# Retention and two feed-forward layers on one core: the double-bank PSUM tiles get a pool of their own, and four single-bank tiles follow them

## The chip, the cores and the metric

The kernel runs on one core of a Trainium2 chip. The metric is the time of one execution on the device in microseconds (us). Several runs are given by their median, and the profile is of one execution.

## What is computed

The reference, cut to what matters:

```python
def _attn_ref(q, k, v):                       # 4 x 8 x 576 x 64, fp32
    scores = (1.0 / np.sqrt(D_)) * np.matmul(q, k.transpose(0, 1, 3, 2))
    gamma = 1.0 - 2.0 ** (-5.0 - np.arange(H, dtype=np.float32))
    Dmat = np.where(rel >= 0, gamma[:, None, None] ** rel[None, :, :], 0.0)
    return np.matmul(scores * Dmat[None, :, :, :], v)
...
x = attn_out.transpose(0, 2, 1, 3).reshape(B * S, H * D)      # 2304 x 512
h = x @ w_in;  x = (h * (1.0 / (1.0 + np.exp(-h)))) @ w_out   # layer 1, 512 -> 2048 -> 512
h = x @ w_in2; g = np.maximum(h, 0.0) + alpha * np.minimum(h, 0.0)
out = g @ w_out2                                              # layer 2
```

## The kernel before

Retention (an attention with a fixed decay in place of a softmax) is worked out in 18 blocks of 128 rows, with a state that is carried from block to block. The two layers then take the 2304 rows as three pieces of 768, each in two halves of 384 columns. fp32 values are split into a high and a low part (`split`), and each product is three matmuls of parts.

The layers run in 24 steps: 8 groups of hidden features (`GROUPS`, four for each layer) times the three pieces. The first two steps are interleaved with the last blocks of retention; `close_att` closes retention's pools after them, and the 22 steps after it are the layers alone. A step has two calls of `unit`, each of which forms two blocks of 128 hidden features for both halves by a scheme of Strassen's kind with seven products instead of eight. A product is 6 matmuls of 384 columns. In the order of the code they are A11 (into a tile a), S1 (into d), A12 (a), S2 (b), S4 (d), S3 (b) and A22 (b). Between them the kernel reads partial sums out: ScalarE (ACT) copies a into b after A11, d into s5 after S1, b into s2 after S2; VectorE (DVE) adds s2 to d after S4, and reads b after S3; `activate` reads a, d, s5 and b. Between the products of `unit` the calls `fill(...)` put pieces of the second matmul (`y_pieces` in layer 1, `out_pieces` in layer 2), which accumulate into a tile o and are added to `ybuf` by DVE or copied there by ACT.

PSUM has eight banks of 2 KiB for each partition. Four of them are tiles of one bank (`banks`). The other four are two tiles of two banks each, `xo` and `sd` (`two`), which retention uses whole. `homes` says which places a, b, d and o rotate through; `close_att` appends the halves of `sd` to b and d and the halves of `xo` to o:

```python
    homes = {"a": banks[0:1], "b": banks[1:2], "d": banks[2:3], "o": banks[3:4]}
    ...
        homes["b"].append(two["sd"][:, 0])
        homes["d"].append(two["sd"][:, 1])
        homes["o"] += [two["xo"][:, i] for i in range(2)]
```

So from `close_att` on, every second unit has b and d in the two halves of `sd`, and o goes round banks[3] and the halves of `xo`.

The order of the instructions on each engine is set by the class `Program`: all calls are recorded first, and `order` lists them by estimated start times. PE's order stays as it is written. Dependences are kept by PSUM bank there (`grains`). The semaphores that hold the engines to the data's order are put in by the framework afterwards, from the tiles that each instruction reads and writes. All operations are issued by one helper line, L222, so rows of the profile are told apart by their tiles.

Of the kernel before, what the change touches and what calls it, by code (L numbers as in the profile page):

```python
# [9 lines left out]
F32 = mybir.dt.float32  # L10
# [8 lines left out]
P = 128  # L19
# [206 lines left out]
def retention_ffn_kernel(ctx: ExitStack, tc: tile.TileContext, qkv, w1, w2, alpha, small, out):  # L226
# [4 lines left out]
    ps = ctx.enter_context(tc.tile_pool(name="ps", bufs=1, space=bass.MemoryType.PSUM))  # L231
# [43 lines left out]
    rings["act"].grow(big, "act", HALF, 7)  # L275
    xops = [big.tile([P, 4 * HALF], F32R, name=f"xop{i}") for i in range(7)]
    banks = [ps.tile([P, 512], F32, name=f"bank{i}") for i in range(4)]
    two = {k: ps.tile([P, 2 * 512], F32, name=k).rearrange("p (b t) -> p b t", b=2) for k in ("xo", "sd")}
    homes = {"a": banks[0:1], "b": banks[1:2], "d": banks[2:3], "o": banks[3:4]}

    att_pool = ctx.enter_context(ExitStack())
    att = att_pool.enter_context(tc.tile_pool(name="att", bufs=1))
    packs = [att.tile([P, 4 * DM], F32, name=f"pack{i}") for i in range(PACKS)]
    late_x = ybuf[:, (NPR - 1) * NC * 2 * HALF:]
    packs.append(late_x[:, 0:4 * DM])
# [14 lines left out]
    def close_att():  # L300
        nc.issue()
        att_pool.close()
        pool = ctx.enter_context(tc.tile_pool(name="layers", bufs=1))
        rings["w0"].grow(pool, "w0b_", 14 * 2 * P, 1, F32R)
        rings["w1"].grow(pool, "w1b_", 512, 6, F32R)
        stock.free += [pool.tile([P, HALF], F32R, name=f"gb{i}") for i in range(6)]
        rings["act"].grow(pool, "actb", HALF, 3)
        rings["raw"].grow(pool, "rawb", 512, 1, I64)
        homes["b"].append(two["sd"][:, 0])
        homes["d"].append(two["sd"][:, 1])  # L310
        homes["o"] += [two["xo"][:, i] for i in range(2)]

    def pack(n):
        at = n % (PACKS + 1) if n < EARLY else (n - EARLY) % PACKS
# [376 lines left out]
    for n, (gi, layer, qs, p) in enumerate(steps):  # L691
# [14 lines left out]
        if with_blocks:  # L706
            weights(0, 0)
            if n == 0:
                begin_banks()
            old, queue[:] = queue[:], more_blocks(BPP // 2)  # L710
            for i, e in enumerate(old):
                queue.insert(2 * i, e)
            unit(layer, qs[0], (gi, p), fill, (1, 1, 1, 1, 1, len(queue)))
            queue += more_blocks(BPP // 2)
            unit(layer, qs[1], (gi, p), fill, (0, 1, 0, 1, 0, 1))
            if n == NPR - 2:
                close_att()
                begin_banks()
                nc.sync.dma_start(out=alpha_sb, in_=alpha)
                nc.vector.tensor_scalar(out=nalpha_sb, in0=alpha_sb, scalar1=-1.0, scalar2=1.0, op0=ALU.mult,  # L720
                                        op1=ALU.add)
            else:
                homes["o"].append(banks[0])
            queue += now
            fill(len(queue))
            queue += then
            if n < NPR - 2:
                del homes["o"][1:]
            continue
# [68 lines left out]
```

## Time and profile before

| | |
|---|---|
| median of 3 runs | 929.79 us (929.47 to 930.74) |
| the profiled execution | 929.9 us, of which the span of its instructions is 928.0 us |
| PE busy | 836.5 us (90%) |
| DVE busy | 566.1 us (61%) |
| ACT busy | 487.6 us (53%) |
| DMA queue of the program | 45.7% of 16 engines' time |

PE is TensorE's matmul stream and PEld its weight loads, which run beside it. Matmuls are pipelined, so the rows of two neighbours overlap. Where a row has a time in brackets with an arrow, the engine sat idle that long before it, and the arrow names the engine and tile whose work ended the wait.

### The profile page before, as it was taken

What the parts mean: (1) busy time and instruction counts of PE and PEld (TensorE: products, weight loads), DVE (VectorE), ACT (ScalarE), POOL (GpSimd) and SP (SyncE); (2) the same over time, 40 slices, a digit from 0 to 9 for tenths busy, and PEclk for the clock granted to TensorE, in tenths of its full rate; (3) what the DMA queues carried; (4) which work ended last, traced back from release to release, by engine and by line L of the source; (5) the groups of instructions that cost most, each with busy time, mean ns of one, the idle gap of its engine ahead of it and who ended that gap; (6) DMA issues with size and microseconds to landing.
All of it is one profiled execution on the core that took longest, in us unless ns stands there. A gap on an engine that the chain in (4) does not pass through costs nothing.

```text
span 928.0 us, 15112 instructions
## 1 busy us (share of the span) xinstructions
PE 836.5 (90%) x6222; PEld 755.9 (81%) x6222; DVE 566.1 (61%) x985; ACT 487.6 (53%) x910; POOL 0.2 (0%) x4
## 2 busy tenths in 40 slices
PE   4778999898998999999998998998998998998998
PEld 3667989898998998988997887887886887887886
DVE  5799768767266533763266887685466843643533
ACT  2657468887456633574364677785245632432331
POOL 0000000000000000000000000000000000000000
PEclk9689999999999999999999999999999999999999
DMA  8786738265603851163632645254601733024711
GB/s 328 274 331 212 287 134 304 91 221 213 269 1 98 321 183 56 46 242 142 227 146 94 262 148 203 69 218 179 238 1 45 283 111 128 1 100 183 283 46 69
DMA packets 35637, 157.49 MB, mean 170 GB/s; under 512 B 4080, under 2 KB 4336, under 8 KB 35568
## 3 DMA queue, kind: packets, MB, share of 16 engines
q1 hardware_dynamic: 35568, 156.52, 45.7%
q8 instruction: 49, 0.80, 0.3%
q14 instruction: 20, 0.16, 0.1%
HBM read 118.76 MB, written 37.75 MB: 169 GB/s over the span
## 4 chain that ended last, share of the span: by engine, by line
PE 85%; DVE 5%; ACT 5%; DMA 3%; issue 2%; SPq 0%; DVEq 0%; ACTq 0%
PE bank L222 39%; PE xo L222 29%; PE sd L222 16%; DMA rawb<-in_w 2%; DVE ybuf L222 2%; ACT act L222 1%; ACT sd L222 1%; DMA pack<-in_qkv 1%; ACT ybuf L222 1%; ACT actb L222 1%; DVE act L222 0%; DVE actb L222 0%; ACT top L222 0%; DVE sd L222 0%; ACT low L222 0%
## 5 line engine op out<-in xcount | busy, mean ns | idle before, releaser
L222 PE MATMUL bank<-xop,w 128*128 128x384 f32 x997 | 197.5, 338 | 4.6 <-DVE act L222 3.4
L222 PEld LDWEIGHTS bank<-xop,w 128*128 128x128 f32 x997 | 175.6, 189 | 10.9 <-DVE act L222 2.3
L222 PE MATMUL sd<-xop,w 128*128 128x384 f32 x391 | 87.2, 348 | 21.9 <-ACT act L222 7.8
L222 DVE TENSOR_TENSOR ybuf<-xo,ybuf 128x384 f32<-128x384 f32 (+2 forms) x85 | 52.0, 612 | 83.0 <-PE xo L222 83.0
L222 PEld LDWEIGHTS sd<-xop,w 128*128 128x128 f32 x391 | 67.0, 188 | 36.8 <-ACT act L222 13.8
L222 PE MATMUL xo<-w,g 128*128 128x512 f32 (+1 forms) x273 | 71.8, 392 | 4.7 <-DVE ybuf L222 4.7
L222 PE MATMUL sd<-xop,w0b 128*128 128x384 f32 x270 | 60.8, 349 | 15.9 <-ACT sd L222 5.0
L222 PE MATMUL xo<-g,w 128*128 128x384 f32 x315 | 66.7, 338 | 5.7 <-DVE ybuf L222 3.9
L222 PE MATMUL bank<-xop,w0b 128*128 128x384 f32 x360 | 70.9, 335 | 0.0
L222 DVE TENSOR_TENSOR g<-act,g 128x384 fp32r<-128x384 f32 x103 | 56.6, 553 | 22.9 <-ACT g L222 22.4
L222 PEld LDWEIGHTS sd<-xop,w0b 128*128 128x128 f32 x270 | 46.3, 188 | 27.0 <-ACT act L222 8.0
L222 PEld LDWEIGHTS bank<-xop,w0b 128*128 128x128 f32 x360 | 63.6, 188 | 1.9
L222 ACT CAST g<-act 128x384 fp32r<-128x384 f32 x103 | 52.7, 513 | 20.8 <-DVE act L222 19.2
L222 PEld LDWEIGHTS xo<-g,w 128*128 128x128 f32 x315 | 55.2, 188 | 8.9 <-DVE ybuf L222 5.8
L222 PEld LDWEIGHTS xo<-w,g 128*128 128x128 f32 x273 | 49.8, 188 | 15.1 <-DVE ybuf L222 7.3
L222 ACT ACTIVATE act<-bank 128x384 f32<-128x384 f32 x66 | 32.4, 491 | 53.5 <-PE bank L222 42.1
L222 PE MATMUL bank<-g,w 128*128 128x384 f32 x273 | 56.3, 344 | 1.6 <-DVE g L222 1.5
L222 PEld LDWEIGHTS bank<-g,w 128*128 128x128 f32 x273 | 49.1, 193 | 2.9 <-DVE g L222 2.3
L222 PE MATMUL xo<-w1b,g 128*128 128x512 f32 x168 | 45.3, 397 | 4.4 <-DVE ybuf L222 2.4
L222 ACT COPY ybuf<-xo 128x256 f32<-128x256 f32 (+2 forms) x58 | 25.2, 434 | 39.8 <-PE xo L222 38.3
L222 PE MATMUL xo<-g,w1b 128*128 128x384 f32 x204 | 44.1, 336 | 2.0 <-DVE ybuf L222 2.0
L222 ACT ACTIVATE low<-low,seven 128x512 int32<-128x512 f32 x64 | 44.7, 720 | 0.3
(109 smaller groups left out, 1383.1 us busy)
## 6 DMA issues: line engine op xcount, KB each, us to landing
xop<-od SPq DMA_DIRECT2D x84, 768.0 KB, 6.5
od<-xop SPq DMA_DIRECT2D x42, 768.0 KB, 4.3
pack<-in_qkv SPq DMA_DIRECT2D x32, 512.0 KB, 6.2
raw<-in_w SPq DMA_DIRECT2D x32, 512.0 KB, 4.4
rawb<-in_w SPq DMA_DIRECT2D x28, 512.0 KB, 4.1
out<-ybuf SPq DMA_DIRECT2D x17, 256.0 KB, 2.0
ybuf<-in_qkv SPq DMA_DIRECT2D x4, 512.0 KB, 8.7
ybuf<-in_w SPq DMA_DIRECT2D x4, 512.0 KB, 8.8
```

Source lines behind the costliest of these rows:

```text
L222: getattr(getattr(self.nc, name), method)(*args, **kwargs)
```

## The change

`xo` and `sd` come from a new PSUM pool, which is opened and closed together with retention's buffers. When it has been closed, `close_att` opens another pool with four tiles of one bank each, `late0` to `late3`, and appends those to b, d, o and o.

```diff
     banks = [ps.tile([P, 512], F32, name=f"bank{i}") for i in range(4)]
-    two = {k: ps.tile([P, 2 * 512], F32, name=k).rearrange("p (b t) -> p b t", b=2) for k in ("xo", "sd")}
     homes = {"a": banks[0:1], "b": banks[1:2], "d": banks[2:3], "o": banks[3:4]}
...
     att = att_pool.enter_context(tc.tile_pool(name="att", bufs=1))
+    att_ps = att_pool.enter_context(tc.tile_pool(name="att_ps", bufs=1, space=bass.MemoryType.PSUM))
+    two = {k: att_ps.tile([P, 2 * 512], F32, name=k).rearrange("p (b t) -> p b t", b=2) for k in ("xo", "sd")}
...
-        homes["b"].append(two["sd"][:, 0])
-        homes["d"].append(two["sd"][:, 1])
-        homes["o"] += [two["xo"][:, i] for i in range(2)]
+        late_ps = ctx.enter_context(tc.tile_pool(name="late_ps", bufs=1, space=bass.MemoryType.PSUM))
+        for i, k in enumerate("bdoo"):
+            homes[k].append(late_ps.tile([P, 512], F32, name=f"late{i}"))
```

The order of the instructions stays as it was on every engine; what differs are the semaphores that they wait for. The pieces below are rows of PE, with the waits named, from the step that the profile of before shows from 811 us on: w0b holds the weights, xop_154 is the operand of S1, xop_155 of A12, xop_156 of S2, xop_157 of S4 and xop_158 of S3; the numbers behind a name only tell buffers apart. In the changed program late_1927 is b, late_1928 is d, late_1929 and late_1930 are o. A wait names the engine, not the instruction, and one that an engine has already waited out isn't named again.

PE at A11 (bank_160), S1 and the piece after it, before:

```order
L222 MATMUL bank_160<-xop_153,w0b_1903 128x384 x6
L222 MATMUL sd<-xop_154,w0b_1903 128x384 x2
L222 MATMUL sd<-xop_154,w0b_1903 128x384 [waits Activation_49]
L222 MATMUL sd<-xop_154,w0b_1903 128x384 x3
L222 MATMUL xo<-w_6_128,gb_1910 128x512 [waits DVE_49]
L222 MATMUL xo<-w_7_129,gb_1910 128x512
```

and in the changed program, up to A12:

```order
L222 MATMUL bank_160<-xop_153,w0b_1907 128x384 x6
L222 MATMUL late_1928<-xop_154,w0b_1907 128x384 x6
L222 MATMUL late_1929<-w_6_128,gb_1914 128x512 [waits DVE_49]
L222 MATMUL late_1929<-w_7_129,gb_1914 128x512
L222 MATMUL late_1929<-w_6_128,gb_1915 128x512
L222 MATMUL late_1929<-w1b_1908,g_134 128x512
L222 MATMUL late_1929<-w1b_1909,g_134 128x512
L222 MATMUL late_1929<-w1b_1908,g_135 128x512
L222 MATMUL bank_160<-xop_155,w0b_1907 128x384 [waits Activation_49]
```

S1's third matmul waited for ACT; now S1 is one row, and the wait for ACT's copy out of bank_160 stands where A12 writes that bank again.

PE at S2 and S4, before, and in the changed program:

```order
L222 MATMUL sd<-xop_156,w0b_1903 128x384 [waits Activation_49]
L222 MATMUL sd<-xop_156,w0b_1903 128x384 x5
L222 MATMUL sd<-xop_157,w0b_1903 128x384 x2
L222 MATMUL sd<-xop_157,w0b_1903 128x384 [waits Activation_49]
L222 MATMUL sd<-xop_157,w0b_1903 128x384 x3
```

```order
L222 MATMUL late_1927<-xop_156,w0b_1907 128x384 x6
L222 MATMUL late_1928<-xop_157,w0b_1907 128x384 [waits Activation_49]
L222 MATMUL late_1928<-xop_157,w0b_1907 128x384 x5
L222 MATMUL late_1930<-w_6_128,gb_1914 128x512 [waits DVE_49]
L222 MATMUL late_1930<-w_7_129,gb_1914 128x512
```

S4's third matmul waited for ACT's copy out of b; now only its first one waits, for ACT's earlier copy out of d.

PE at S3 and up to A22 (xop_159), before, and in the changed program:

```order
L222 MATMUL sd<-xop_158,w0b_1903 128x384 [waits Activation_49]
L222 MATMUL sd<-xop_158,w0b_1903 128x384 [waits DVE_49]
L222 MATMUL sd<-xop_158,w0b_1903 128x384 x4
L222 MATMUL xo<-w1b_1906,g_140 128x512
L222 MATMUL xo<-w1b_1907,g_140 128x512
L222 MATMUL xo<-w1b_1906,g_141 128x512
L222 MATMUL xo<-w1b_1908,g_132 128x512
L222 MATMUL xo<-w1b_1909,g_132 128x512
L222 MATMUL xo<-w1b_1908,g_133 128x512
L222 MATMUL sd<-xop_159,w0b_1903 128x384 [waits DVE_49]
```

```order
L222 MATMUL late_1927<-xop_158,w0b_1907 128x384 [waits Activation_49]
L222 MATMUL late_1927<-xop_158,w0b_1907 128x384 x5
L222 MATMUL late_1930<-w1b_1910,g_140 128x512
L222 MATMUL late_1930<-w1b_1911,g_140 128x512
L222 MATMUL late_1930<-w1b_1910,g_141 128x512
L222 MATMUL late_1930<-w1b_1912,g_132 128x512
L222 MATMUL late_1930<-w1b_1913,g_132 128x512
L222 MATMUL late_1930<-w1b_1912,g_133 128x512
L222 MATMUL late_1927<-xop_159,w0b_1907 128x384 [waits DVE_49]
```

S3's second matmul waited for DVE's activation, which reads d; now its first one waits for ACT's copy out of b alone. The wait for DVE ahead of A22 is there in both: DVE reads b after S3.

## Rows read from the trace of the kernel before

**Rows 1.** The page: span, and the granted clock in 40 slices.

```profile
span 928.0 us, 15112 instructions
...
PEclk9689999999999999999999999999999999999999
```

**Rows 2.** Stretches: length, PE, PEld, DVE, ACT, POOL busy (instructions), clock, DMA share, GB/s.

```profile
133.00:220.00 87.00, 80.34 (x445) 76.22 (x444) 62.53 (x107) 70.44 (x127) 0.00 (x0) 1.00 0.60 218
155.00:175.00 20.00, 18.78 (x106) 17.85 (x105) 17.41 (x32) 18.31 (x35) 0.00 (x0) 1.00 0.32 106
470.00:570.00 100.00, 92.42 (x475) 83.12 (x474) 79.01 (x127) 64.16 (x114) 0.00 (x0) 1.00 0.49 187
540.00:560.00 20.00, 19.22 (x96) 17.02 (x95) 18.54 (x30) 15.96 (x29) 0.00 (x0) 1.00 0.57 198
812.00:847.00 35.00, 32.53 (x156) 27.94 (x156) 15.86 (x27) 11.15 (x24) 0.00 (x0) 1.00 0.48 175
133.00:928.00 795.00, 733.43 (x3784) 662.69 (x3782) 466.07 (x813) 417.91 (x772) 0.00 (x0) 1.00 0.42 154
```

**Rows 3.** PE's waits, 133 to 928 us: total us, times, longest.

```profile
PE xo L222 <- DVE ybuf L222: 15.6, 22, 0.8
PE sd L222 <- ACT act L222: 12.6, 24, 0.6
PE sd L222 <- ACT sd L222: 12.6, 22, 0.9
PE sd L222 <- ACT actb L222: 4.6, 10, 0.6
PE sd L222 <- DVE actb L222: 4.5, 6, 0.8
PE xo L222 <- ACT ybuf L222: 4.4, 7, 0.7
PE sd L222 <- DVE act L222: 3.6, 5, 0.8
PE bank L222 <- DVE act L222: 0.7, 1, 0.7
```

**Rows 4.** Timeline of PE, one step: start, us, instruction [idle before, releaser].

```profile
812.07 0.98 PE L222 MATMUL sd<-xop,w0b 128*128 128x384 f32 x4 [0.55 <-ACT sd L222]
...
815.33 1.55 PE L222 MATMUL xo<-w1b,g 128*128 128x512 f32 x6
...
818.84 0.97 PE L222 MATMUL sd<-xop,w0b 128*128 128x384 f32 x4 [0.57 <-ACT act L222]
...
822.21 1.15 PE L222 MATMUL sd<-xop,w0b 128*128 128x384 f32 x5 [0.71 <-DVE act L222]
...
824.59 1.20 PE L222 MATMUL sd<-xop,w0b 128*128 128x384 f32 x6
...
830.49 3.29 PE L222 MATMUL bank<-xop,w 128*128 128x384 f32 x18
...
842.67 1.19 PE L222 MATMUL xo<-w,g 128*128 128x512 f32 x4 [0.78 <-DVE ybuf L222]
...
847.21 0.98 PE L222 MATMUL sd<-xop,w0b 128*128 128x384 f32 x4 [0.55 <-ACT sd L222]
```

**Rows 5.** Timeline of ACT and DVE in the same step.

```profile
811.55 0.46 ACT L222 COPY sd<-bank 128x384 f32<-128x384 f32 x1 [4.92 <-PE sd L222]
...
818.31 0.48 ACT L222 COPY act<-sd 128x384 f32<-128x384 f32 x1 [1.10 <-PE sd L222]
...
821.54 0.61 DVE L222 SCALAR_TENSOR_TENSOR act<-act,nalpha_sb,sd 128x384 f32<-128x384 f32 x1 [1.06 <-PE sd L222]
...
823.40 0.56 DVE L222 TENSOR_TENSOR act<-sd,act 128x384 f32<-128x384 f32 x1 [1.24 <-PE sd L222]
```

**Rows 6.** Tile sd, 133 to 928 us: min/median/max ns, first and last start.

```profile
L222 PE MATMUL sd<-xop,w x391: 333/334/446, 133.2 to 790.3; 128*128 128x384 f32 x196
```

## The prediction

> **What bounds the kernel now.** I read the page first, then the stretches, PE's waits, and one step of the steady part instruction by instruction.
>
> The page gives the span and the granted clock [rows 1]: 928.0 us, and a clock that dips only in the first slices, where retention runs alone, and stands at the top digit from there on. The stretches [rows 2] show that from 133 us on, when the retention part is over and its pool is closed, PE is busy in 733.43 of 795.00 us, at a granted share of 1.00 (2.4 GHz), while DVE has 466 and ACT 418 us of work there and the DMA engines are at 0.42. So PE is the bound for 795 of 928 us, and what can be won is PE's idle time.
>
> The waits [rows 3] say where that idle time is. Nearly all of it stands ahead of matmuls into sd and xo, the two double-bank tiles: 12.6 + 12.6 + 4.6 + 4.5 + 3.6 = 37.9 us in 67 waits ahead of sd, 15.6 + 4.4 = 20.0 us in 29 waits ahead of xo, and 0.7 us in one wait ahead of all four single-bank tiles together. The single-bank tiles are used in the same way by the same code, so the two kinds of tile differ, not the work. No row names a DMA.
>
> One step shows why [rows 4, 5]. At 811.55 ACT copies bank0 into the first half of sd (unit's b). PE, which is by then writing S1 into the second half (d), stands still and goes on at 812.07, right after that copy ends at 812.01. S1 has no use for b. At 818.84 the same again: PE waits for ACT's copy out of b (818.31, 0.48 us) before it goes on writing d. At 822.21 the roles are swapped: PE writes b and waits for DVE's activation (821.54, 0.61 us), which reads d. At 842.67 PE writes one half of xo and waits for DVE's add out of the other half. In each case the engines are on different banks of one tile: the wait is for the tile, not for the bank.
>
> **What the change does, part by part.**
>
> *Order.* The recorder's order is not moved: it already keyed PSUM by the 2 KiB bank, so the halves of a double tile were two things to it. On each engine the instructions of the changed program stand in the order of before; PE has 2439 rows both ways when waits are left out. With waits shown PE's rows fall from 2906 to 2812, because products that were cut by a wait in their middle become one row. The three places shown in the section on the change are the stalls at 812.07, 818.84 and 822.21.
>
> *Waits removed.* I set the wait list of every PE instruction after 133 us beside the times of the trace. All 96 waits ahead of sd and xo [rows 3] are of this kind: in the changed program they are gone, or they ask for something that had ended long before PE got there. The one wait ahead of a single-bank tile stays.
>
> *Price of one.* The idle time in the rows is not the whole price. Matmuls overlap: 18 in a row take 3.29 us [rows 4], so (3.29 - 0.334) / 17 = 0.174 us from start to start, while one lasts 0.334 [rows 6]. A stall therefore also loses the overlap, 0.334 - 0.174 = 0.160. And the first matmul after a stall lasts 0.446, the maximum in [rows 6], which is 0.112 more. For the 512-column ones six take 1.55 us [rows 4]; their interval comes out at about 0.23 and the loss the same. So a stall costs its idle time plus 0.27 us.
>
> *Sum.* 57.9 + 96 x 0.27 = 83.8 us. One steady step as a check: from 812.07 to 847.21 are 35.14 us [rows 4], with four stalls of 0.57, 0.71, 0.78 and 0.55; they cost 2.61 + 4 x 0.27 = 3.69, and a step without them takes 31.4 us.
>
> *What takes their place.* Where a stall goes, the next true dependence decides. In the steady step that is the last product on b (A22, 824.59), which must wait for DVE's read of b; that read starts at 823.40 and lasts 0.56 [rows 5], so it is over 0.63 us before PE comes. DVE starts it when S3 is done, and S3 moves with PE, so this 0.6 us of cover moves along and isn't spent. Room on the engines: in the step DVE has 15.86 and ACT 11.15 us of work for 35 us [rows 2], and still only that for 31.4. So I take the whole gain in the steady steps.
>
> In two stretches there is less room, because weights are decoded and operands are split there. At 155 to 175 ACT is busy 18.31 of 20 us, at 540 to 560 DVE 18.54 of 20 [rows 2]. Take 2 or 3 stalls (0.87 us each on average) out of 20 us and the busiest engine has next to nothing left; PE will then meet waits that the stalls now cover. The 0.7 us wait of a single-bank tile [rows 3] is of this kind already. I estimate 2 us given back in each, 4 in all, between 0 (all is kept) and the 20 us of the second rival below.
>
> *Waits added.* The new pool may hand out the banks only when the old tiles' last users are done. It does so once, at 133 us, where PE's first write to the new b waits for ACT's last copy of retention's output; that is one wait of the length of those above at most, and I take 0. ACT and DVE lose such waits too (the copy at 811.55 was itself held by S1's first matmuls into the other half), which can add 1 to 3 us of gain at the low end. SP's queue is neither reordered nor given a wait.
>
> By the profiled execution's own time, 929.9 us (span 928.0 and 1.9 around it; the median of the runs is 929.79): 929.9 - 83.8 + 4 = 850 us.
>
> **Rivals.**
>
> *The wait only moves.* PE would be held at the same places by whoever feeds it, and nothing changes: 930 us. It would take a supplier with as much work as PE; the fullest, DVE, has 466 us for 795 [rows 2], and PE stalls on nothing but these tiles, so little speaks for it. Part of this is the same outcome if the removed waits weren't what held PE. [...]
>
> *The full stretches keep their stalls.* If in 133 to 220 and 470 to 570 ACT and DVE, at 70.44 of 87 and 79.01 of 100 us [rows 2], set the pace, nothing is won in 187 of 795 us: 83.8 x 187 / 795 = 20 us less gain, 866 us. For it: both are in-order and near full in parts of these stretches. Against: over the whole stretches their work fits, with 91 us left for the 79 even after a tenth is taken off.
>
> *Slower: the clock.* If PE's granted clock fell from 2.4 to 1.2 GHz once it is never idle, a 384-column matmul would cost up to 0.174 us more. The gain of 83.8 is used up when 83.8 / 0.174 = 480 of the 3784 matmuls [rows 2] run so; beyond that the kernel is slower than before, and with 1000 of them it would take 846 + 174 = 1020 us. Against: in [rows 1] the low digits stand in the first slices, where PE works least, and the share is 1.00 in every stretch after 133 us, up to PE's densest. Another way to get slower is hard to see, since orders are kept and waits go.
>
> **How the numbers follow.** The forecast, 850 with its own range 843 to 858, has 0.84; the full stretches, around 866, 0.11; the wait that only moves 0.03; the clock 0.02. The range 842 to 864 takes in the forecast with the gain of ACT and DVE at its low end and most of the second rival at its high end. This kernel's runs spread from 929.47 to 930.74, so changes under 0.2% can't be told from none: faster by more 0.95, within it 0.03, slower 0.02.
>
> **What would show it.** PE's waits from about 133 us on: the rows ahead of the late tiles should shrink from 57.9 us to under 6, mostly in the stretches of decoding. A steady step should take 31.3 to 31.6 us in place of 35.14, with 18 matmuls still in 3.29 us and the clock share at 1.00. The stretch up to 133 us should stay as long as it is. PE's busy share should rise to 98% and more after 133 us, DVE's and ACT's work should keep its sum. The prediction is wrong if rows of waits as long as these stand ahead of other tiles, if the matmul interval has grown, or if the first 133 us have changed.

## The result and the profile after

The changed kernel takes 843.26 us in the median of 4 runs (842.25 to 845.98) where the kernel before takes 929.63 us beside it: a ratio of 0.9075, with a 95% interval of 0.9049 to 0.9100. The forecast was 850, in a range of 842 to 864.

The page of the changed kernel, span and granted clock, answers to [rows 1]:

```profile
span 842.4 us, 15109 instructions
...
PEclk9789999999999999999999999999999999999999
```

Its stretches answer to [rows 2], with the same columns:

```profile
133.00:153.00 20.00, 20.00 (x117) 20.00 (x116) 15.29 (x22) 16.47 (x30) 0.00 (x0) 1.00 0.85 323
153.00:173.00 20.00, 19.34 (x110) 18.63 (x109) 18.42 (x36) 19.74 (x38) 0.00 (x0) 1.00 0.40 138
505.00:525.00 20.00, 20.00 (x102) 17.91 (x101) 18.75 (x31) 17.51 (x32) 0.00 (x0) 1.00 0.89 341
133.00:842.40 709.40, 705.29 (x3783) 666.81 (x3781) 463.74 (x813) 414.93 (x772) 0.00 (x0) 1.00 0.47 172
```

After 133 us PE is busy in 705.29 of 709.40 us, 99%, where it was 92%. DVE's and ACT's work is what it was (463.74 and 414.93 us against 466 and 418), in a shorter time. The clock's share is unchanged at 1.00. PE's waits after 133 us are one row, where [rows 3] has eight:

```profile
PE bank L222 <- DVE act L222: 0.7, 1, 0.7
```

That is the one wait that was there before the change too. The step that [rows 4] shows from 811 us on, in PE's timeline of the changed kernel (start, us, instruction):

```profile
736.84 1.23 PE L222 MATMUL bank<-xop,w0b 128*128 128x384 f32 x6
737.91 1.20 PE L222 MATMUL late<-xop,w0b 128*128 128x384 f32 x6
...
742.77 2.25 PE L222 MATMUL late<-xop,w0b 128*128 128x384 f32 x12
...
746.24 1.21 PE L222 MATMUL late<-xop,w0b 128*128 128x384 f32 x6
...
748.68 1.21 PE L222 MATMUL late<-xop,w0b 128*128 128x384 f32 x6
...
754.58 3.29 PE L222 MATMUL bank<-xop,w 128*128 128x384 f32 x18
...
763.97 2.92 PE L222 MATMUL late<-w,g 128*128 128x512 f32 x12
...
768.09 1.23 PE L222 MATMUL bank<-xop,w0b 128*128 128x384 f32 x6
```

and ACT and DVE in it, which answer to [rows 5]:

```profile
738.11 0.46 ACT L222 COPY late<-bank 128x384 f32<-128x384 f32 x1 [3.50 <-PE bank L222]
...
744.07 0.48 ACT L222 COPY act<-late 128x384 f32<-128x384 f32 x1 [0.80 <-PE late L222]
...
746.25 0.61 DVE L222 SCALAR_TENSOR_TENSOR act<-act,nalpha_sb,late 128x384 f32<-128x384 f32 x1 [0.56 <-ACT act L222]
...
747.49 0.56 DVE L222 TENSOR_TENSOR act<-late,act 128x384 f32<-128x384 f32 x1 [0.62 <-PE late L222]
```

S1 (737.91) is one row of six, and ACT's copy of bank0 into b runs at 738.11, inside it. S2 and S4 are one row of twelve (742.77): the wait between them is gone, while ACT copies b at 744.07. S3 (746.24) starts while DVE works on d (746.25). From one A11 to the next are 768.09 - 736.84 = 31.25 us, where the step took 35.14 and the prediction had 31.3 to 31.6. Eighteen matmuls take 3.29 us as before.

### The profile page after: what moved, and what is told of

Same layout as the page of the kernel before. It is cut to its first block, busy times and chain, and to the rows that moved or that the text cites. A ratio compares the mean times of both kernels' runs of the same rounds, so it can differ in the third digit from the quotient of the medians.

```text
span 842.4 us, 15109 instructions
## 1 busy us (share of the span) xinstructions
PE 807.1 (96%) x6222; PEld 758.4 (90%) x6222; DVE 564.0 (67%) x985; ACT 484.9 (58%) x910; POOL 0.2 (0%) x4
## 4 chain that ended last, share of the span: by engine, by line
PE 87%; DVE 5%; DMA 3%; issue 2%; ACT 2%; SPq 0%; DVEq 0%
PE bank L222 42%; PE late L222 41%; PE xo L222 2%; DMA rawb<-in_w 2%; PE sd L222 2%; DMA pack<-in_qkv 1%; DVE wt L222 1%; DVE xop L222 1%; DVE ybuf L222 1%; DVE att L222 1%; DVE wk L222 0%; DVE pack L222 0%; DMA alpha_sb<-in_alpha 0%; ACT ybuf L222 0%; DVE w L222 0%
## 5 line engine op out<-in xcount | busy, mean ns | idle before, releaser
L222 DVE TENSOR_TENSOR ybuf<-late,ybuf 128x384 f32<-128x384 f32 (+2 forms) x85 | 52.0, 611 | 56.7 <-PE late L222 56.4
L222 PE MATMUL late<-xop,w 128*128 128x384 f32 x391 | 76.4, 334 | 0.0
L222 PEld LDWEIGHTS late<-xop,w 128*128 128x128 f32 x391 | 68.9, 188 | 1.6
L222 PE MATMUL late<-w,g 128*128 128x512 f32 (+1 forms) x273 | 69.9, 389 | 0.0
L222 PE MATMUL late<-g,w 128*128 128x384 f32 x315 | 64.4, 335 | 0.0
L222 PEld LDWEIGHTS late<-w,g 128*128 128x128 f32 x273 | 50.2, 188 | 8.2
L222 PEld LDWEIGHTS late<-g,w 128*128 128x128 f32 x315 | 55.4, 188 | 0.4 <-DVE g L222 0.3
L222 PE MATMUL late<-xop,w0b 128*128 128x384 f32 x270 | 52.8, 335 | 0.0
L222 PEld LDWEIGHTS late<-xop,w0b 128*128 128x128 f32 x270 | 47.6, 188 | 1.5 <-DVE act L222 0.2
L222 PE MATMUL late<-w1b,g 128*128 128x512 f32 x168 | 43.6, 393 | 0.0
```

Source lines behind the costliest of these rows:

```text
L222: getattr(getattr(self.nc, name), method)(*args, **kwargs)
```

## The experiments

The theory is that of the prediction: PE waits for a tile where it needs a bank, and one such wait costs its idle time plus 0.27 us. The ratios are to the kernel before, timed in the same rounds. The idle time in each sum below is read from that kernel's own trace; what the sum tests is the 0.27 us and that nothing else costs or gains. PE's order is the same in all of them.

**Only b and d in single-bank tiles.**

```diff
-        for i, k in enumerate("bdoo"):
-            homes[k].append(late_ps.tile([P, 512], F32, name=f"late{i}"))
+        pair = late_ps.tile([P, 2 * 512], F32, name="pair").rearrange("p (b t) -> p b t", b=2)
+        homes["o"] += [pair[:, i] for i in range(2)]
+        for i, k in enumerate("bd"):
+            homes[k].append(late_ps.tile([P, 512], F32, name=f"late{i}"))
```

> The new pool as in the change, but only b and d get a bank of their own; the two extra places of o are the halves of one double-bank tile again. Theory (PE waits for a tile where it needs only a bank, and each such wait costs its idle time plus 0.27 us): the 67 waits ahead of sd go, the 29 ahead of xo come back, 20.0 + 29 x 0.27 = 27.8 us, so 843.3 + 27.8 = 871 us. Rival (the pool: closing it and placing the banks anew is what gained): 843 us. Rival (one kind of wait set the pace, the other was in its shadow): within 5 us of 843 or of 930.

Measured: 871.0 us (869.56 to 873.32), ratio to before 0.9386 (0.9360 to 0.9412). Its waits of PE after 133 us:

```profile
PE pair L222 <- DVE ybuf L222: 15.7, 22, 0.8
PE pair L222 <- ACT ybuf L222: 4.4, 7, 0.7
PE bank L222 <- DVE act L222: 0.7, 1, 0.7
```

The 29 waits of xo are back and no other. They are priced at 20.1 + 29 x 0.27 = 27.9 us, which with 843.3 makes 871.2.

**Only o in single-bank tiles.** The same with the roles changed: `pair` for b and d, two tiles of one bank for o.

> The counterpart: the two extra places of o are single-bank tiles, b and d share one double-bank tile of the new pool. Theory: 67 waits come back, 37.9 + 67 x 0.27 = 56.0 us, so 899 us, and the two gains add up to the whole. Rival (pool): 843 us. Rival (one kind sets the pace): within 5 us of 843 or of 930, and the two gains don't add up.

Measured: 903.52 us (901.05 to 903.89), ratio 0.9728 (0.9703 to 0.9754). PE's waits ahead of `pair`:

```profile
PE pair L222 <- ACT pair L222: 14.1, 22, 1.7
PE pair L222 <- ACT act L222: 12.6, 24, 0.6
PE pair L222 <- ACT actb L222: 4.6, 10, 0.6
PE pair L222 <- DVE actb L222: 4.5, 6, 0.8
PE pair L222 <- DVE act L222: 3.6, 5, 0.8
```

The 67 waits are back, 39.4 us of idle time: 39.4 + 67 x 0.27 = 57.5, which makes 900.8. The measured time is 2.7 us more. Between the profiled executions of this kernel and of the changed one lie 903.88 - 844.24 = 59.6 us, 2.1 more than priced; 1.7 of these lie ahead of the layers, whose first matmul on b starts at 134.8 us where it is 133.1 with the change. The gains of the two halves, 57.8 and 25.2 us against their own runs of before (928.75), add up to 83.0 of the 86.4 of the whole change; neither stands in the other's shadow.

**The new pools, but two double-bank tiles in them, b with d and o with o.**

```diff
-        for i, k in enumerate("bdoo"):
-            homes[k].append(late_ps.tile([P, 512], F32, name=f"late{i}"))
+        pairs = [late_ps.tile([P, 2 * 512], F32, name=f"pair{i}").rearrange("p (b t) -> p b t", b=2) for i in range(2)]
+        for i, k in enumerate("bdoo"):
+            homes[k].append(pairs[i // 2][:, i % 2])
```

> The pools are opened and closed as in the change, and the late places are in new tiles, but in two of two banks each, b with d and o with o, as before. Theory: all 96 waits are back, 929 to 931 us. Rival (pool): 843 us.

Measured: 927.57 us (925.73 to 931.38), ratio 0.9994 (0.9977 to 1.0011): no gain clear of noise. PE's waits are those of [rows 3] within 0.2 us a row, 57.7 us in 96. So the pools, their closing and the banks' new places gained nothing that shows here, and cost nothing either.

**The old pool and tiles, but b shares a tile with one place of o, and d with the other.**

```diff
         homes["b"].append(two["sd"][:, 0])
-        homes["d"].append(two["sd"][:, 1])
-        homes["o"] += [two["xo"][:, i] for i in range(2)]
+        homes["d"].append(two["xo"][:, 0])
+        homes["o"] += [two["sd"][:, 1], two["xo"][:, 1]]
```

> The kernel before with its pool and its two double-bank tiles; only who shares a tile is changed: b with one place of o, d with the other. Theory: S1 and S4 no longer wait for work on b, nor one place of o for the other; other waits come, where a piece of the second matmul writes o while b or d of the same tile is being read. Set beside the trace of the changed kernel some 50 waits in place of 96 would be late there, so about half of the gain: 870 to 900 us. Rival (pool): 930 us, since the pool is the old one.

Measured: 892.45 us (890.86 to 893.77), ratio 0.9614 (0.9588 to 0.9640). PE's waits after 133 us:

```profile
PE xo L222 <- DVE xo L222: 10.2, 14, 0.7
PE sd L222 <- DVE ybuf L222: 8.9, 12, 0.8
PE xo L222 <- ACT act L222: 5.8, 8, 1.7
PE xo L222 <- ACT actb L222: 3.5, 6, 0.6
PE sd L222 <- DVE act L222: 3.1, 4, 1.1
PE sd L222 <- ACT ybuf L222: 1.9, 3, 0.7
PE xo L222 <- DVE act L222: 0.9, 2, 0.8
PE bank L222 <- DVE act L222: 0.7, 1, 0.7
PE sd L222 <- DVE actb L222: 0.7, 1, 0.7
PE sd L222 <- ACT sd L222: 0.6, 1, 0.6
PE xo L222 <- DVE actb L222: 0.2, 1, 0.2
```

The waits have changed their partners with the tiles: xo now waits for DVE's add into d (DVE xo), sd for the add out of o (DVE ybuf). Without the row of bank they are 35.8 us in 52, priced at 35.8 + 52 x 0.27 = 49.8, which makes 893. With no pool, no bank and no order changed, 36 us were to be had (928.75 - 892.45) by choosing whom a tile is shared with.

**One and two more reads of b.** These two test the cover that the prediction left in a step: DVE's read of b behind S3 is over 0.6 us before A22 writes b. The added reads are work whose result isn't used. `order`, which goes by estimated start times, also puts some of ACT's and DVE's other instructions in another order in these two kernels.

```diff
+    spare = big.tile([P, HALF], F32, name="spare")
...
         product(b, both, S3, T3)
+        for _ in range(1):
+            nc.vector.tensor_tensor(out=spare, in0=b, in1=s5, op=ALU.add)
         nc.vector.tensor_tensor(out=s5, in0=b, in1=s5, op=ALU.add)
```

> The changed kernel with one more read of b by VectorE (an add into a spare tile, about 0.56 us, its result unused) ahead of each read of b behind S3. It puts off the moment from which A22 may write b. Theory (0.6 us of cover between that read and A22 is left in the changed kernel, so one such read is still hidden): 843 to 848 us. Rival (the cover was spent when the stalls went, so that the next dependence is already the bound): 0.56 + 0.27 us at each of the 22 units with a late b at least, 861 us or more.

Measured: 846.32 us (844.34 to 848.17), ratio 0.9100 (0.9081 to 0.9119). PE's waits after 133 us are 1.2 us ahead of a single-bank tile, in the one place that waited before, and 0.2 us in one wait ahead of a late tile. From the first matmul on a late tile (133.4 us) to the end the profiled execution takes 710.7 us, with the change 709.3: the cover held 44 more reads of 0.56 us.

> The same with two more reads (1.12 us). Theory: in the 22 units with a late b the 0.6 us of cover is overdrawn by 0.5 us, which costs 0.5 + 0.27 us each, 17 us; in the other 22 units the cover is about 1.1 us and just holds or costs a few us: 858 to 870 us. Rival (the cover was spent): twice 0.56 + 0.27 at 22 units or more, 874 us or more. If it stays under 850 us, there is more cover than the theory has.

Measured: 862.0 us (860.8 to 865.36), ratio 0.9275 (0.9252 to 0.9297). The rows of PE's waits that lead, and one place in the timeline of all engines (idle time and releaser in brackets):

```profile
PE late L222 <- DVE act L222: 5.0, 10, 0.8
PE bank L222 <- DVE act L222: 1.8, 1, 1.8
PE late L222 <- DVE actb L222: 1.5, 3, 0.6
```

```profile
698.13 1.15 DVE L222 TENSOR_TENSOR spare<-late,actb 128x384 f32<-128x384 f32 x2 [0.63 <-PE late L222]
699.31 0.56 DVE L222 TENSOR_TENSOR actb<-late,actb 128x384 f32<-128x384 f32 x1
...
699.92 1.33 PE L222 MATMUL late<-xop,w 128*128 128x384 f32 x6 [0.44 <-DVE actb L222]
```

A22 now waits 0.44 us for the last read of b. The added reads put that one off by 1.18 us (698.13 to 699.31); less the 0.44 and the 0.16 of lost overlap that is 0.58, so the cover was the 0.6 us of the theory. The total came out as expected, but not for the count given, so that it lies in the range is in part luck: such waits are 13, not 22, twelve of them once a step from 471 us on and one at 220 us, since in most of layer 1's units the cover is larger. The named rows price at 8.3 us of idle time and 14 x 0.27, 12 us, of which 1 is the wait that was there before.

The clock has a part in the rest. Just behind the wait of 1.8 us its share is 0.51, the level of 1.2 GHz, for 169.0 to 172.5 us (the columns of [rows 2], and PE's timeline):

```profile
169.00:172.50 3.50, 3.50 (x13) 3.50 (x13) 2.85 (x5) 2.61 (x5) 0.00 (x0) 0.51 0.00 0
```

```profile
167.83 1.33 PE L222 MATMUL bank<-xop,w 128*128 128x384 f32 x6 [1.83 <-DVE act L222]
169.00 2.08 PE L222 MATMUL late<-g,w 128*128 128x384 f32 x6
170.87 1.94 PE L222 MATMUL bank<-g,w 128*128 128x384 f32 x6
172.65 1.22 PE L222 MATMUL late<-g,w 128*128 128x384 f32 x6
```

From 169.00 to 172.65 twelve matmuls take 3.65 us, where the changed kernel has 2.39 for the same twelve (168.56 to 170.95): 1.3 us. Some 6 us of the 18.7 are left, which were not followed further.

**Late tiles for o alone.** b and d keep one place each; two banks lie unused. Here too `order` moves some of ACT's and DVE's instructions.

```diff
-        for i, k in enumerate("bdoo"):
+        for i, k in enumerate("oo"):
```

> The changed kernel with late tiles for o alone: b and d keep one place each (banks[1], banks[2]) and two banks of PSUM stay unused. Theory (what counted was that b and d did not share a tile, not how many places they rotate through; within a unit all products on b and d go to one place anyway): 843 to 852 us, with at most short waits for the last reads of b and d by the unit before. Rival (the second place of b and d is what keeps PE from waiting): 44 units with waits of the length seen, 0.87 us each, 880 us or more.

Measured: 843.69 us (842.79 to 849.66), ratio 0.9093 (0.9057 to 0.9130): the time of the changed kernel. PE's waits after 133 us:

```profile
PE bank L222 <- ACT bank L222: 0.8, 1, 0.8
PE bank L222 <- DVE act L222: 0.7, 1, 0.7
```

The second place of b and d is worth one wait of 0.8 us. Where b and d shared a tile, these places came with waits that cost some 57 us.

## Why the prediction was right, and where a size was off

*The wait is for the tile.* Right. With the pools of the change and tiles of two banks all 96 waits return (927.57 us); with the old pool and other partners they change partners (892.45 us).

*The price of one, idle time plus 0.27 us.* Right to within 0.02 us. Set on 843.3 us, it gives 871.2, 900.8, 926.9 and 893 us for four kernels that have 29, 67, 96 and 52 of the waits; measured were 871.0, 903.5, 927.6 and 892.5. That the first matmul after a stall is longer shows in the row of [rows 6] too: without stalls its maximum falls from 446 to 340. It isn't such stalls alone that do it, since another row of the late tiles, which has no wait in the rows of waits, keeps a maximum of 446:

```profile
L222 PE MATMUL late<-xop,w x391: 333/334/340, 133.1 to 718.3; 128*128 128x384 f32 x196
L222 PE MATMUL late<-g,w x315: 334/334/446, 135.4 to 470.5; 128*128 128x384 f32 x158
```

*The sum, 83.8 us.* The profiled executions differ by 929.9 - 844.24 = 85.7 us, 0.89 for each of the 96 waits instead of 0.87. After 133 us PE's idle time fell from 61.57 to 4.11 us, by 57.5, as the sum has it; its busy time fell by 733.43 - 705.29 = 28.1 us, 0.29 for each wait instead of 0.27. One thing that the sum left out is a matmul that is late and long with no idle time ahead of it, and so stands in no row of waits. S3's first one in the step of [rows 4] is such a one (821.06, 0.44 us long), which the changed kernel doesn't have (746.24); how much of the 0.02 they make wasn't worked out. The stretch up to 133 us has not changed: the first matmul on the late b starts at 133.1, with no wait ahead of it, where [rows 6] has 133.2.

*4 us given back in the full stretches.* This is the term that was mis-sized: nothing was given back. PE waits only the 0.7 us that it waited before. At 153 to 173 us ACT is busy 19.74 of 20 us, more than the 18.31 that made me doubt [rows 2], and PE still runs 19.34; at 505 to 525 us DVE is busy 18.75 of 20 and PE all 20. So a nearly full ACT or DVE didn't hold PE here, but for that one wait: their results came in time. How long before PE's reading they were ready wasn't measured, other than the 0.6 us at A22. These 4 us are the larger part of the 6.7 between the 850 of the forecast and the 843.3 measured, which lies only 1.3 above the low end of the range; 1.9 are the price, and 1 is that the profiled execution (844.24) lies above the median.

*The cover of 0.6 us at A22 moves along.* Right: one more read of b is hidden, two are not. In the step of the changed kernel DVE's read ends at 747.49 + 0.56 = 748.05, and A22 starts at 748.68, 0.63 later, as before.

*The rivals.* That the wait only moves is refuted by the one row of waits left; that the full stretches keep their stalls, by the same row. The clock did not fall: its share is 1.00 and the matmul interval has kept its length. Against this rival the prediction said that the low digits stand where PE works least, which the trace doesn't bear out: before the change PE was busy 9.71 of the first 23 us at a share of 1.00, and 17.14 of the next 23 at 0.63. The one fall between 133 us and the last 3 us in any of these profiles is that of the kernel with two more reads, and it stands behind a long wait, not where PE has none.

## What to carry to other kernels

Look at which tile a wait names on both sides: where PE writes one part of a tile and the releaser reads or writes another, the wait belongs to the allocation, and a tile for each bank removes it, or better chosen partners remove a part. Price a stall of a dense matmul stream by more than its idle time in the rows; here it was 0.27 us more. A supplier that is busy for 90% and more of its time need not give a gain back: here none was. Look at how long its results lie before they are read, as at A22.

## What was not expected

The first 133 us, in which PE's work is the same in every kernel here, vary from one execution to the next: the layers' first matmul on a late tile starts at 133.1 us with the change, at 131.0 in the kernel with b and d alone in single-bank tiles, and at 134.8 in that with o alone. The granted clock varies in this stretch and, the fall at 169 us of the kernel with two more reads apart, nowhere else before the last 3 us. But its shares don't order these starts: for 46 to 70 us it is 0.86 in the first two, which are 2.1 us apart, and 0.79 in the last. In the four runs of the changed kernel the mean share was 0.990 and 0.988 at 842.25 and 842.29 us, 0.988 at 844.24 and 0.982 at 845.98. The starts differ by as much as these four runs do (3.8 and 3.7 us), so this stretch may make most of their spread; neither that nor the clock as its cause is shown.
